# Hash masks of a fused attention kernel: 64-row products with zeros in place of 32-row products

## The chip, the cores and the metric

The kernel runs on one core of a Trainium2 chip. The metric is the device time in microseconds (us), the median of several runs. The engines are called as in the profile: PE is TensorE (PEld its weight loads), DVE is VectorE, ACT is ScalarE, POOL is GpSimd, and SP issues most DMA transfers.

## The reference

Two blocks follow each other. The first is attention with hash buckets: a query and a key meet only if the signs of six random projections agree. The second is a Fourier mixing with an MLP.

```python
q_bits = (einsum('bhsd,dk->bhsk', q, proj) > 0)       # 6 bits per query; the same for k
mask = q_bucket[:, :, :, None] == k_bucket[:, :, None, :]
scores = where(mask, q @ k.T / sqrt(D), -1e9)
attn = softmax(scores); x = attn @ v                  # heads side by side: (B, S, 512)
u = x + real(fft2(x)); un = layernorm(u)
out = u + relu(un @ w_ch1) @ w_ch2
```

Here B = 4, H = 8 heads, S = 768, D = 64, and all inputs are fp32, with 512 x 2048 and 2048 x 512 weights that arrive as 64-bit numbers and are narrowed on the chip.

## The kernel before

Heads are worked in pairs: pair `n` holds two heads on partitions 0 to 63 and 64 to 127, and there are 16 pairs, four for each batch. Queries and keys of a pair lie transposed in `qt` and `kt` (128 x 768). A pair is worked in six key chunks of 128 keys. For a chunk, `weigh` makes the scores for the two query halves `g` (384 queries each): two products on 64 rows of fp32, one for each head, into one of two PSUM buffers `sc` (L885), and the exponential on ACT into `pk` (L889), of which there are two. `values` multiplies the chunk before with the values into `oo` (L906). DVE adds up `pk` into `acc` (L980). After the last chunk, products with ones make the sums (L924), and `scale` divides: DVE turns the sums (L931), takes reciprocals, ACT copies them (L940), DVE turns back and multiplies (L941, L945).

Pairs 0 to 4, called LITE, get their mask on PE. `prepare` makes the sign bits of queries and keys in `qk`, bf16 (L794 products, L798 comparisons). The numbers are such that the product of query bits with key bits is zero where all six agree and hugely negative elsewhere, and it is added to the scores in PSUM by a product ahead of the score product (L878). Bits have 7 rows of use in a block of 32 partitions. Before, block `j` is query or key half `g = j // 2` of head `j % 2`, so the masks of half `g` for the two heads are two products on 32 rows each, at rows `64 g` and `64 g + 32`. Query bits are multiplied by 2**34 (L803). For the keys of the other half, two copies of 64 partitions exchange the blocks of the two halves (L806). The later pairs are masked on DVE by comparing bucket numbers (L895).

The order in each engine's queue is fixed in the program; each engine works its queue in order and waits at semaphores. The part up to the end of batch 0's attention and `pwf` (L1483) is in an order written by hand (a manual schedule). In batch 0, attention is interleaved with the arrival of the first weight matrix: each of 16 slices comes by DMA (`zraw`, `fraw`, L687) and is narrowed by DVE (L633, L637, L643) and ACT (L641, L648, L649); for half of them column means are made (`average`: `ws` L658, `part` L663, `wm` L666) and taken off (L672). From batch 1 on, attention is interleaved with the mixing of the batch before (`cs` L1078, `A` and `B` L1107) and its MLP (`h_p` L1382, `o` L1262). Pair 4 is the first of batch 1. `bt` L821 is the first step of pair 5's bits.

The preparation of pair `n + 1` is advanced one step in each chunk of pair `n` from the second on, so DVE works on bits between accumulation and conversion:

```python
for io, nm in enumerate("qk"):
    ps = pt([P, HALF], f"bits{nm}{n}")
    for j in range(4):
        g, h = divmod(j, 2)
        nc.tensor.matmul(ps[32 * j : 32 * j + 32, :], pjw[:, h * D : h * D + 32], ...)
```

Of the kernel before, what the change touches and what calls it, by code (L numbers as in the profile page):

```python
# [11 lines left out]
F32 = mybir.dt.float32  # L12
# [5 lines left out]
ALU = mybir.AluOpType  # L18
AX = mybir.AxisListType

P = 128
B, H, S, D = 4, 8, 768, 64
# [5 lines left out]
HALF = S // 2  # L28
# [10 lines left out]
BIG = 2.0**34  # L39
# [10 lines left out]
def _consts():  # L50


    s = np.arange(HALF)
    freq = np.concatenate([2 * np.arange(NK), 2 * np.arange(NK) + 1])
    ang = 2.0 * np.pi * (np.outer(s, freq) % S) / S
    seq = np.stack([np.cos(ang), np.sin(ang)])
    seq = seq.reshape(2, NT // 2, P, 2 * NK).transpose(2, 0, 1, 3)


    d = np.arange(DM // 2)  # L60
    ang = 2.0 * np.pi * (np.outer(d, np.arange(DM)) % DM) / DM
    sin = -np.sin(ang)
    sin[0] = 1.0 - 2.0 * (np.arange(DM) % 2)
    chan = np.concatenate([np.cos(ang), sin]).reshape(NDC, P, DM).transpose(1, 0, 2)

    off = np.zeros((P, 2))
    for h in range(2):
        off[h * D : h * D + NBITS] = 0.5  # L70
        off[h * D + NBITS] = (NBITS / 4.0, -1.0)


    pw = np.zeros((P, 2, P))
    for r in range(P):
        h, bit = divmod(r % 32, NBITS)
        if h < 2:
            pw[r, h] = 2.0**bit


    d = np.arange(DM // 2)
    fr = np.concatenate([np.arange(DM // 2 + 1), np.arange(1, DM // 2)])
    ang = 2.0 * np.pi * (np.outer(d, fr) % DM) / DM
    ch = np.where(np.arange(DM) <= DM // 2, np.cos(ang), np.sin(ang))
    ch = ch.reshape(2, P, DM // 2, 2).transpose(1, 0, 3, 2)

    s = np.concatenate([np.arange(2, HALF // 2, 2), np.arange(1, HALF // 2, 2)])  # L90
    rows = np.concatenate([s, [0, HALF // 2], s])
    kind = np.repeat([0, 1, 2, 3], [len(s), 1, 1, len(s)])
    sq = np.zeros((2, 2, P, HALF + 1))
    for par in range(2):
        cols = slice(par * NK, HALF + 1 if par else NK)
        ang = 2.0 * np.pi * (np.outer(rows, freq[: HALF + 1][cols]) % S) / S
        for k in range(2):
            own = kind == (0 if par == k else 3)
            own |= (kind == 1) & (k == 0) | (kind == 2) & (k == par)
            w = np.where(own[:, None], np.sin(ang) if k else np.cos(ang), 0.0)  # L100
            w = w.reshape(NT // 2, P, -1)
            sq[0, k, :, cols] = w[0 if par == k else 2]
            sq[1, k, :, cols] = w[1]
    sq = sq.transpose(2, 0, 1, 3)
    return {
        "pw": np.ascontiguousarray(pw, dtype=np.float32),
        "ch": np.ascontiguousarray(ch, dtype=np.float32),
        "sq": np.ascontiguousarray(sq, dtype=np.float32),
        "seq": np.ascontiguousarray(seq, dtype=np.float32),
        "chan": np.ascontiguousarray(chan, dtype=np.float32),  # L110

        "off4": np.ascontiguousarray(np.tile(off[:32], (4, 1)), dtype=np.float32),
        "off": np.ascontiguousarray(off, dtype=np.float32),
    }

# [366 lines left out]
def _main(  # L482
# [13 lines left out]
    nc = tc.nc  # L496

    const = ctx.enter_context(tc.tile_pool(name="const", bufs=1))
# [39 lines left out]
    def load(n, names="qkv", second=nc.sync):  # L538

        b, t = divmod(n, NPAIR)
        for nm in names:
            src = {"q": q, "k": k, "v": v}[nm]
            tag, bufs = ("vn", 2) if nm == "v" else ("qkn", 2)
            tl = wt([P, S], F32, tag, f"{nm}n{n}", bufs)
            nat[nm, n] = tl
            if nm == "v" or n == 0:  # L550
                tc_ = tl.rearrange("p (c h d) -> p c h d", c=NT, h=2)
                for h in range(2):
                    s = src[b, 2 * t + h]
                    s = (
                        s.rearrange("(p c) d -> p c d", c=NT) if nm == "q"
                        else s.rearrange("(c p) d -> p c d", p=P)
                    )
                    (second if h else nc.sync).dma_start(tc_[:, :, h, :], s)
                continue
            for i in range(4):  # L560
                s = src[b, 2 * t + i // 2, :, i % 2 * 32 : i % 2 * 32 + 32]
                d = tl[32 * i : 32 * i + 32]
                if nm == "k":
                    nc.sync.dma_start(
                        d.rearrange("p (j a) -> p j a", a=32),
                        s.rearrange("(j b) a -> b j a", b=32),
                    )
                else:
                    s = s.rearrange("(j b r) a -> r b j a", b=32, r=2)
                    d = d.rearrange("p (r j a) -> r p j a", r=2, a=32)  # L570
                    for r in range(2):
                        nc.sync.dma_start(d[r], s[r])
# [14 lines left out]
        nc.sync.dma_start(pjw[h * D : (h + 1) * D, h * D : h * D + NBITS], proj)  # L587
    off = const.tile([P, 2], F32, tag="off", name="off")
    nc.sync.dma_start(off, cn["off4"].ap())
    load(0, "v")  # L590
    pj = const.tile([P, 32], F32, tag="pj", name="pj")
    nc.gpsimd.memset(pj, 0.0)
# [156 lines left out]
    def prepare(n):  # L749
# [3 lines left out]
        for io, nm in enumerate("qk"):  # L753
            tn = nat.pop((nm, n))
            tt = wt([P, S], F32, nm + "t", f"{nm}t{n}")
            if n > 0:
                to, at = tt, tn
                if nm == "q":

                    to = tt.rearrange("p (i r n) -> p r i n", i=2, r=2)  # L760
                    at = tn.rearrange("p (r i n) -> p r i n", i=2, r=2)
# [21 lines left out]
        if lite:  # L783

            qk = wt([P, 2, S], BF16, "qb", f"qkb{n}")
            bits = {"q": qk[:, 0, 0:HALF], "k": qk[:, 1, 0:HALF]}
            for io, nm in enumerate("qk"):  # L790
                ps = pt([P, HALF], f"bits{nm}{n}")
                for j in range(4):
                    g, h = divmod(j, 2)
                    nc.tensor.matmul(  # L794
                        ps[32 * j : 32 * j + 32, :], pjw[:, h * D : h * D + 32],
                        ts[nm][:, g * HALF : (g + 1) * HALF], start=True, stop=True,
                    )
                nc.vector.tensor_scalar(  # L798
                    bits[nm], ps, 0.0, off[:, io : io + 1],
                    op0=ALU.is_gt, op1=ALU.subtract,  # L800
                )
                if io == 0:
                    nc.vector.tensor_scalar(bits[nm], bits[nm], BIG, None, op0=ALU.mult)  # L803
                else:
                    for g in range(2):
                        nc.vector.tensor_copy(  # L806
                            qk[g * D : (g + 1) * D, 1, HALF:S],
                            qk[(1 - g) * D : (2 - g) * D, 1, 0:HALF],
                        )
                yield  # L810
            preps[n] = ts["q"], ts["k"], qk, None
            return
# [50 lines left out]
    def weigh(n, c):  # L863

        qt, kt, qb, kb = preps[n]
        ks = slice(c * P, (c + 1) * P)
        heads = [slice(h * D, (h + 1) * D) for h in range(2)]
        pk = pks[npk[0] % NPK]
        npk[0] += 1
        for g in range(2):  # L870
            qs = slice(g * HALF, (g + 1) * HALF)
            ps = ps_sc.tile([P, 2, 512], F32, tag="sc", name=f"sc{n}_{g}_{c}")
            if kb is None:

                at = (c + (NT // 2 if g else 0)) % NT * P
                for h in range(2):
                    rows = slice(g * D + 32 * h, g * D + 32 * h + 32)
                    nc.tensor.matmul(  # L878
                        ps[:, h, 0:HALF], qb[rows, 1, at : at + P], qb[rows, 0, 0:HALF],
                        start=True, stop=False,  # L880
                    )

            for h, rows in enumerate(heads):
                with behind() if g + h and n >= NPAIR else nullcontext():
                    last[0] = nc.tensor.matmul(  # L885
                        ps[:, h, 0:HALF], kt[rows, ks], qt[rows, qs],
                        start=kb is not None, stop=True,
                    )
            nc.scalar.activation(  # L889
                pk[:, g, :, 0:HALF], ps[:, :, 0:HALF], AF.Exp, scale=SCALE  # L890
            )
        if kb is not None:
            for h in range(2):
                w = pk[:, :, h, 0:HALF]
                nc.vector.scalar_tensor_tensor(  # L895
                    w, qb[:, h].rearrange("p (g s) -> p g s", g=2), kb[:, h, c : c + 1], w,
                    op0=ALU.is_equal, op1=ALU.mult,
                )
        return pk
# [260 lines left out]
    at = NR * 2 * P  # L1160
# [425 lines left out]
```

## Time and profile before

| | |
|---|---|
| time, median of 3 runs | 1102.68 us (1102.34 to 1106.73) |
| profiled execution, span from first to last instruction | 1100.83 us |
| its own time around the span | not recorded apart; the median of the runs is 1.85 us above the span |
| PE busy | 1054.5 us, 96% of the span |
| DVE busy | 786.5 us, 71% |
| ACT busy | 500.6 us, 45% |
| mask products L878 | 120, of 331 ns each, first at 11.0 us, last at 152.3 us |
| score products L885 | 768 records, two passes for one fp32 product |
| granted PE clock | 0.995 of full |

Busy time is the union of the records of an engine. On PE the start of a record is where it began to stream, while its end is modelled and overlaps the next one; so steps between starts are the time that a product costs, and a busy PE is not a PE at its peak. Idle time ahead of an instruction is put down to the semaphore that came last.

### The profile page before, as it was taken

To read this page: it belongs to the slowest core of one execution; us is meant where nothing else is said; L and a number is where in the kernel's file an instruction comes from. 1 tells how busy PE (TensorE), PEld (TensorE's weight loads), DVE (VectorE), ACT (ScalarE), POOL (GpSimd) and SP (SyncE) were. 2 spreads that over 40 slices of the span, in tenths; PEclk is the share of its full clock that TensorE was granted. 3 is DMA by queue.
4 is the path that set the end of the run, shared out by engine and by line. 5 is a ranking of instruction groups with operands and counts; after the bars stand their busy time and mean duration, and the time that the engine had idled before them with its cause. 6 is when DMAs were issued, how large, how long until landed. Compare 5 with 4: busy or idle time off the path is not lost.

```text
span 1100.8 us, 14127 instructions
## 1 busy us (share of the span) xinstructions
PE 1054.5 (96%) x4933; PEld 629.4 (57%) x4933; DVE 786.5 (71%) x1321; ACT 500.6 (45%) x1055; POOL 58.6 (5%) x132
## 2 busy tenths in 40 slices
PE   7999997999989999999999999999999999999996
PEld 2333354446744675545664576645674569768675
DVE  5798958868699977776767785965856785644353
ACT  6888555653276324454326433355315522340420
POOL 0000000002000020010000011001000002100000
PEclk9999999999999999999999999999999999999998
DMA  8745443441056161322144134213032205122401
GB/s 224 221 90 119 76 123 88 149 147 26 20 139 210 46 204 34 66 61 70 26 157 108 48 73 162 44 39 96 15 121 75 68 24 172 54 82 85 126 20 41
DMA packets 175566, 103.13 MB, mean 94 GB/s; under 512 B 129408, under 2 KB 162816, under 8 KB 175488
## 3 DMA queue, kind: packets, MB, share of 16 engines
q1 hardware_dynamic: 169696, 88.65, 29.9%
q0 software_dynamic: 4224, 13.11, 3.8%
q8 instruction: 41, 0.67, 0.3%
q10 hardware_dynamic: 1568, 0.39, 0.2%
q14 instruction: 37, 0.30, 0.1%
HBM read 81.14 MB, written 20.97 MB: 93 GB/s over the span
## 4 chain that ended last, share of the span: by engine, by line
PE 63%; DVE 11%; ACT 4%; DMA 2%; issue 2%; DVEq 0%; SPq 0%; ACTq 0%
PE o L1262 22%; PE h_p L1382 21%; PE oo L906 7%; PE sc L885 6%; DVE pk L895 3%; PE cs L1078 2%; PE A L1107 2%; DMA zraw<-in_moe_w_ch_dram 2%; PE B L1107 1%; DVE acc L980 1%; ACT rr L940 1%; PE bits L817 1%; DVE w L1274 1%; DVE h L1248 1%; PE un L1133 1%
## 5 line engine op out<-in xcount | busy, mean ns | idle before, releaser
L1262 PE MATMUL o<-w,h 128*128 128x256 f32 x1152 | 259.4, 382 | 1.2 <-ACT tq L1281 0.7
L1262 PEld LDWEIGHTS o<-w,h 128*128 128x128 f32 x1152 | 216.3, 190 | 43.6 <-issue 4.6
L889 ACT ACTIVATE pk<-sc 128x768 f32<-128x768 f32 x192 | 148.5, 809 | 81.6 <-PE sc L885 64.5
L1382 PE MATMUL h_p<-x,w 128*128 128x384 f32 x448 | 163.1, 494 | 3.2 <-ACT h L1404 1.7
L885 PE MATMUL sc<-qt,kt 64*128 64x384 f32 x768 | 159.8, 519 | 5.4 <-ACT pk L889 5.1
L906 PE MATMUL oo<-pk,vn 128*64 128x385 f32 (+1 forms) x768 | 155.1, 499 | 4.0 <-DVE pk L895 3.3
L895 DVE SCALAR_TENSOR_TENSOR pk<-qb,kb,pk 128x768 f32<-128x768 bf16 x132 | 129.0, 1013 | 29.5 <-ACT pk L889 29.4
L1382 PEld LDWEIGHTS h_p<-x,w 128*128 128x128 f32 x448 | 82.0, 190 | 70.6 <-ACT pk L889 5.4
L980 DVE TENSOR_TENSOR acc<-acc,pk 128x1536 f32<-128x1536 f32 (+1 forms) x72 | 105.8, 1483 | 6.1 <-ACT pk L889 5.4
L1382 PE MATMUL h_p<-w 128*128 128x384 f32 x288 | 105.5, 489 | 2.3 <-ACT w L1419 2.3
L906 PEld LDWEIGHTS oo<-pk,vn 128*64 128x64 f32 x768 | 49.1, 136 | 97.8 <-issue 68.7
L885 PEld LDWEIGHTS sc<-qt,kt 64*128 64x128 f32 x768 | 62.9, 185 | 56.1 <-issue 29.6
L1382 PEld LDWEIGHTS h_p<-w 128*128 128x128 f32 x288 | 53.7, 190 | 41.7 <-ACT w L1419 3.5
L1292 ACT COPY tq<-o 128x256 f32<-128x256 f32 x24 | 8.9, 373 | 105.1 <-PE o L1262 105.1
L1274 DVE SCALAR_TENSOR_TENSOR w<-o,rs,w 128x256 f32<-128x256 f32 x56 | 26.8, 479 | 41.6 <-PE o L1262 41.6
L1262 PE MATMUL o<-w 128*128 128x256 f32 x176 | 42.3, 383 | 1.4 <-DVE w L1274 1.3
L1408 DVE TENSOR_TENSOR h<-h 128x384 f32<-128x384 f32 x32 | 17.8, 556 | 32.2 <-ACT h L1407 32.2
L1281 ACT COPY tq<-o 128x256 f32<-128x256 f32 x24 | 8.9, 371 | 69.3 <-PE o L1262 69.2
L1262 PEld LDWEIGHTS o<-w 128*128 128x128 f32 x176 | 32.8, 190 | 8.8 <-DVE w L1274 3.0
L1016 POOL DMA_DIRECT2D out_dram<-w x30 | 16.4, 548 | 388.8 <-issue 293.2
L1415 DVE TENSOR_TENSOR h<-h 128x384 f32<-128x384 f32 x32 | 17.7, 553 | 26.9 <-ACT h L1414 26.8
L1308 DVE TENSOR_TENSOR tq<-tq,o 128x256 f32<-128x256 f32 x24 | 10.0, 418 | 34.7 <-PE o L1262 34.7
(170 smaller groups left out, 1329.1 us busy)
## 6 DMA issues: line engine op xcount, KB each, us to landing
w<-ad SPq DMA_DIRECT2D x168, 128.0 KB, 2.0
w<-bd SPq DMA_DIRECT2D x42, 512.0 KB, 4.5
zraw<-in_moe_w_ch_dram POOLq DMA_DIRECT2D x16, 512.0 KB, 4.1
bd<-w SPq DMA_DIRECT2D x14, 512.0 KB, 4.2
vn<-in_v_dram SPq DMA_DIRECT2D x32, 192.0 KB, 3.4
qn<-in_q_dram SPq DMA_DIRECT2D x120, 48.0 KB, 2.4
kn<-in_k_dram SPq DMA_DIRECT2D x60, 96.0 KB, 3.4
zraw<-in_moe_w_ch_dram SPq DMA_DIRECT2D x8, 512.0 KB, 5.7
```

The costliest lines, as they stand in the source:

```text
L885: last[0] = nc.tensor.matmul(ps[:, h, 0:HALF], kt[rows, ks], qt[rows, qs], start=kb is not None, stop=True,)
L889: nc.scalar.activation(pk[:, g, :, 0:HALF], ps[:, :, 0:HALF], AF.Exp, scale=SCALE)
L895: nc.vector.scalar_tensor_tensor(w, qb[:, h].rearrange("p (g s) -> p g s", g=2), kb[:, h, c : c + 1], w, op0=ALU.is_equal, op1=ALU.mult,)
L906: nc.tensor.matmul(oos[g][h * D : (h + 1) * D, 0:w], nat["v", n][:, (2 * c + h) * D : (2 * c + h + 1) * D], pk[:, g, h, 0:w], start=(c == ...
L980: nc.vector.tensor_tensor(acc[:, g], (first if c == 1 else acc)[:, g], new[:, g], op=ALU.add,)
L1078: nc.tensor.matmul(ps[:, pc + 2 * lo : pc + 2 * hi - 1 : 2], z[:, cp, pc, par, t * P : (t + 1) * P], ch[:, cp, pc, lo:hi], start=(cp == 0) ...
L1107: nc.tensor.matmul(ps[:, cols], F[:, par, k, t, j * P : (j + 1) * P], sq[:, t, k, cols], start=(t == 0), stop=(t == 1),)
L1262: nc.tensor.matmul(ps, a[:, r], right7[i][:, r], start=start and r == 0, stop=r == HF // 2 - 1, skip_group_check=not start,)
L1274: nc.vector.scalar_tensor_tensor(t[:, cols], src, r, t[:, cols], op0=ALU.mult, op1=ALU.add)
L1382: nc.tensor.matmul(ps, left[:, k], right[i][:, k], start=start and k == 0, stop=k == 1, skip_group_check=not start,)
L1408: nc.vector.tensor_tensor(c21, c12, c21, op=ALU.add)
L1415: nc.vector.tensor_tensor(c22, c21, c22, op=ALU.add)
```

## The change

The blocks of bits are ordered by head and then by half: block `j` is half `j % 2` of head `j // 2`. A head's two halves now lie on the 64 rows that also hold the head's queries and keys. The mask product of half `g` runs on these 64 rows; the query bits exist twice, `qz[:, 0]` and `qz[:, 1]`, and in version `g` the block of the other half is zero. A new constant `own` (128 x 2, holding 2**34 or 0) is loaded once by SP and is the per-partition scalar of the multiplications: two instead of one for a pair. The exchange of key halves is now between neighbouring blocks of 32 partitions, in four copies instead of two. The comparisons, the number of products and the exponentials are as before.

```diff
+        "own": np.where(np.arange(P)[:, None] // 32 % 2 == np.arange(2), BIG, 0.0),
...
+    own = const.tile([P, 2], F32, tag="own", name="own")
+    nc.sync.dma_start(own, cn["own"].ap())
     load(0, "v")
...
             qk = wt([P, 2, S], BF16, "qb", f"qkb{n}")
-            bits = {"q": qk[:, 0, 0:HALF], "k": qk[:, 1, 0:HALF]}
+            qz = qk[:, 0].rearrange("p (g s) -> p g s", g=2)
+            bits = {"q": qz[:, 0], "k": qk[:, 1, 0:HALF]}
...
-                    g, h = divmod(j, 2)
+                    h, g = divmod(j, 2)
...
                 if io == 0:
-                    nc.vector.tensor_scalar(bits[nm], bits[nm], BIG, None, op0=ALU.mult)
+                    for g in (1, 0):
+                        nc.vector.tensor_scalar(
+                            qz[:, g], qz[:, 0], own[:, g : g + 1], None, op0=ALU.mult
+                        )
                 else:
-                    for g in range(2):
-                        nc.vector.tensor_copy(
-                            qk[g * D : (g + 1) * D, 1, HALF:S],
-                            qk[(1 - g) * D : (2 - g) * D, 1, 0:HALF],
-                        )
+                    for j in range(4):
+                        to, at = (slice(32 * i, 32 * i + 32) for i in (j, j ^ 1))
+                        nc.vector.tensor_copy(qk[to, 1, HALF:S], qk[at, 1, 0:HALF])
...
-                for h in range(2):
-                    rows = slice(g * D + 32 * h, g * D + 32 * h + 32)
+                for h, rows in enumerate(heads):
                     nc.tensor.matmul(
-                        ps[:, h, 0:HALF], qb[rows, 1, at : at + P], qb[rows, 0, 0:HALF],
+                        ps[:, h, 0:HALF], qb[rows, 1, at : at + P],
+                        qb[rows, 0, g * HALF : (g + 1) * HALF],
                         start=True, stop=False,
                     )
```

More of the change, by code (lines that the diff above doesn't have):

```diff
@@ L112, in _consts @@
         "off4": np.ascontiguousarray(np.tile(off[:32], (4, 1)), dtype=np.float32),
+        "own": np.ascontiguousarray(
+            np.where(np.arange(P)[:, None] // 32 % 2 == np.arange(2), BIG, 0.0),
+            dtype=np.float32,
+        ),
         "off": np.ascontiguousarray(off, dtype=np.float32),
```

## The prediction

> **What bounds the kernel now.** I read the page first, for the stage that the change touches. The masked hash products (`L878`) run from 11.0 to 152.3 us of a span of 1100.8, which is slices 1 to 6 of 40.
>
> ```profile
> PE   7999997999989999999999999999999999999996
> ...
> DVE  5798958868699977776767785965856785644353
> ACT  6888555653276324454326433355315522340420
> ```
>
> TensorE (PE) looks full there, but so nearly are ScalarE (ACT, slices 1 to 3) and VectorE (DVE, slices 2 to 3 and 5). Busy time in three windows cut at the events that matter below (window, length, PE, PE weight loads, DVE, ACT) says the same:
>
> ```profile
> 11.00:41.60 30.60, 29.42 (x174) 9.80 (x175) 20.83 (x35) 24.95 (x44) 0.00 (x0) 1.00 0.84 264
> 41.60:95.60 54.00, 52.37 (x317) 17.48 (x316) 48.18 (x76) 48.31 (x96) 0.00 (x0) 1.00 0.50 96
> 95.60:141.70 46.10, 43.76 (x257) 15.77 (x257) 43.59 (x78) 27.85 (x60) 0.11 (x1) 1.00 0.50 111
> ```
>
> From 41.6 to 95.6 three engines share the bound: 52.4, 48.2 and 48.3 of 54.0 us. From 95.6 to 141.7 DVE has 43.6 of 46.1. So the next question is what the PE time is made of; the PE timeline of one key chunk shows it (start, length, group):
>
> ```profile
> 17.13 0.34 PE L878 MATMUL sc<-qkb 32*128 32x384 bf16 x2
> 17.40 0.92 PE L885 MATMUL sc<-qt,kt 64*128 64x384 f32 x4
> 18.25 0.34 PE L878 MATMUL sc<-qkb 32*128 32x384 bf16 x2
> 18.51 0.92 PE L885 MATMUL sc<-qt,kt 64*128 64x384 f32 x4
> 19.36 1.51 PE L906 MATMUL oo<-pk,vn 128*64 128x385 f32 x8
> 20.80 0.34 PE L878 MATMUL sc<-qkb 32*128 32x384 bf16 x2
> ```
>
> A chunk takes 3.67 us: mask pair 0.27, scores 0.85, mask pair 0.26, scores 0.85, values 1.44. Starts are to be trusted, ends overlap. Last, the timelines of DVE and PE, for the places where DVE waits for PE (what PE can give it back) and PE for DVE. The bracket is the idle time before, and its releaser:
>
> ```profile
> 65.11 2.48 DVE L672 TENSOR_TENSOR w<-w,wm 128x512 f32<-128x512 f32 x4 [0.75 <-PE wm L666]
> ...
> 70.23 0.58 DVE L931 STREAM_TRANSPOSE rt<-sum 128x384 f32<-128x384 f32 x1 [0.75 <-PE sum L924]
> ...
> 95.66 0.58 DVE L931 STREAM_TRANSPOSE rt<-sum 128x384 f32<-128x384 f32 x1 [2.30 <-PE sum L924]
> ...
> 121.16 0.98 DVE L941 STREAM_TRANSPOSE rt<-rr 128x768 f32<-128x768 f32 x1 [1.73 <-ACT rr L940]
> ...
> 141.70 1.16 PE L1078 MATMUL cs<-ch,z 128*128 128x127 f32 x8 [1.42 <-DVE bt L821]
> ```
>
> Those four are all the waits over 0.15 us that DVE has from 40.68 to 141.64. At 141.70 PE waits for a DVE queue that has run through since 121.16. This is the ceiling of the whole change.
>
> [...] Inside the 128x128 stream of `L1107` (groups of four passes at 168.89, 169.54, 170.19) a pass of 192 columns takes 0.65/4 = 0.163 us, while the step from its last pass into the 64-row scores takes 0.256: 0.095 of drain. [...] each pass has its own 128-row load, recorded at 190 ns, and still follows in 0.163 us. [...] no 64-row bf16 product runs here. [...]
>
> **The change part by part.**
>
> *TensorE, per chunk.* The counts stay: 120 mask products, two concurrent per half, in 30 chunks. What goes are mode changes, since mask and scores are now both 64 rows by 128. Before, mask to first score pass is 0.262 (0.160 of columns, the rest drain and load); the first score pass takes 0.427 instead of 0.320, since its fp32 weights (0.107 between the two loads of a head) can't be loaded ahead of the change; last pass to next mask is 0.415 (0.320 and 0.095). After: 0.163, 0.323, 0.323 for the first half and 0.163, 0.323, 0.415 for the second, which still leaves the mode for the values; 0.007 more for the first load. Scores and masks of a chunk fall from 2.22 to 1.72, so 0.50 us. Thirty chunks offer 15 us on PE.
>
> *DVE, per pair.* The tile listing gives the prices.
>
> ```profile
> L806 DVE COPY qkb<-qkb x10: 253/255/256, 11.0 to 118.1; 64x384 bf16<-64x384 bf16 x10
> L798 DVE TENSOR_SCALAR qkb<-bitsq,off x5: 611/612/619, 9.5 to 110.5; 128x384 bf16<-128x384 f32 x5
> L803 DVE TENSOR_SCALAR qkb<-qkb x5: 259/260/261, 10.2 to 111.2; 128x384 bf16<-128x384 bf16 x5
> ```
>
> One multiplication more (0.26, with its wait 0.29) and two copies more (2 x 0.255; a copy of 32 partitions has the same 384 elements each): 0.80 per pair, 4.0 in five pairs. [...] the bound is the 0.61 of `L798`, which also takes a per-partition scalar: 0.70 more per pair. Below, an op of 384 elements has no reason to get cheaper than 0.26. I take 0.26.
>
> *SP.* One transfer more (`own`, 1 KB) ahead of `load(0, "v")`. Its neighbour `off` has a 587 ns issue and lands 4.1 us later, so `own` lands near 8.4 and is needed at 10.2. Behind it the value loads, `zraw` and the loads of pair 1 are each issued up to 0.6 later. ACT waits 1.06 for a `zraw` at 23.25, so 0 to 0.6 us is lost; the queue is blocked later anyway (a `qn` issue at 10.19 takes 2.95), I take 0.2. ACT, POOL and the order on PE are unchanged.
>
> *Where the 15 us go.*
> 1. 11.0 to 31.4: the first mask starts 0.30 later (one multiplication ahead of the key bits), its second half waits for four copies, not two; with the cheaper products the scores are ready as before. From 13.36 to 31.39 ACT runs through but for that DMA wait: exponentials and weight conversion, 3.6 us per chunk against PE's 3.67 before. PE only waits more: gain 0.
> 2. 31.4 to 40.68: here ACT idles for PE (0.62, 0.30, and 1.67 until `part` L663). Two chunks in a row are PE's: 0.6 at `part`, 1.1 at the sum that releases DVE at 40.68.
> 3. 40.68 to 95.66: DVE could give back 0.75 + 0.75 + 2.30 = 3.8 and gets 1.6 more work. ACT is tighter. It passes on some 0.65 at `part` 60.41 (the long wait there, 3.42, ends with a PE product that waited 0.92 for DVE `L798`), then 0.19 + 0.17 + 0.31 + 0.30 = 0.97 of waits for PE up to 89.1, and one chunk of PE alone, 0.5. So the sum arrives about 2.0 earlier. DVE would be ready at 93.35 - 1.1 + 0.8 = 93.05, the sum comes at 93.66: 2.0.
> 4. 95.66 to 141.70: DVE runs through, with the ACT round trip of 1.73, which moves along. Nine chunks save 4.5 us on PE and all of it becomes waiting: for `pk`, which DVE frees late, and at `L1078`, whose 1.42 grows. Pair 4's 0.8 is fully exposed: 2.0 - 0.8 = 1.2.
> 5. After 141.70: the last two chunks, at 142.79 and 151.16, are PE's: 1.0. Everything later depends on triggers that move along.
>
> Sum 1.2 + 1.0 - 0.2 = 2.0 us. Against the span of 1100.83 that is 1098.8. The median of the runs lies 1.85 above the span (start and end around it), so **1100.7 us**. A measurement can tell about 0.5%, 5.5 us, from no change.
>
> **The rivals.**
> *DVE and ACT give way (faster).* For it: PE is busy nearly throughout. Against: DVE's waits. If DVE's 3.8 of waits, the 1.73, 1.1 before and 1.0 after are all taken and 2.4 for pairs 2 to 4 paid, that is 5.2 us: 1097.5. More needs DVE to stop being last at 141.70; then up to 15: 1088.
> *Mask products get no cheaper (slower).* If the change from bf16 to fp32 drains as the change of rows does, or the scores' load waits for the mask on the same rows, PE saves nothing. Then DVE's added work decides. Pair 0 adds 0.30 at the start; pairs 1 to 3 fit into DVE's waits; pair 4 adds 0.80 ahead of 141.70; `own` 0.2. That is +1.3: 1104.0, with a slow multiplication +2.3. It decides once PE saves less than 0.8/6 = 0.13 per chunk. Against it: no drain shows within a mode in `L1107`; but both operand types are fp32 there.
> *The two heads' products run one after another (weaker gain).* 60 halves by 0.16 is 9.6 us more on PE, which leaves 5.4 of the 15, 0.18 per chunk: just past that point, about 1103. Against: the 64-row scores of two heads start 7 ns apart.
> *The rows don't change.* Excluded: the products in the changed kernel's instruction order are on 64 rows, all else but the named parts in the same order.
>
> **How the numbers follow.** Forecast 0.65, its own range 1098.5 to 1102.7 (loss at SP 0 to 0.6, slow multiplication, ACT giving back 1 more or less). First rival 0.15, of which 0.10 beyond 5.5 us. No saving 0.17, of which 0.06 beyond 5.5 us, where mask products even become dearer. Serial heads 0.03. So faster 0.10, same 0.84, slower 0.06. The range takes in the first rival's ceiling and the second's price: 1097.0 to 1104.5.
>
> **What would show it.** Right: mask to score about 0.17 and a chunk's products 0.50 shorter; more PE idle before `L878` and at `L1078`; DVE's waits at `L931` shorter; 141.70 moved by about 1. Wrong: mask to score still 0.26 (rival two), or `L1078` reached without a wait for DVE and several us earlier (rival one).

## The result, and the profile after

The changed kernel takes 1102.14 us (median of 20 runs, 1099.91 to 1104.45) beside 1102.88 us for the kernel before (20 runs): a ratio of 0.9993, interval 0.9984 to 1.0002. A second set of runs of it (`e12c_after_again`, below) gives 0.9996, 0.9983 to 1.0009. That is no difference that the measurement can tell: from 1.8 us faster to 0.2 slower, and the forecast gain of 2.0 lies just outside. The span of the profiled execution fell from 1100.8 to 1100.4 us.

TensorE did become cheaper. On the page PE's busy time falls from 1054.5 to 1043.3 us, and slices 3 and 5 of its row are 8 where 9 stood before:

```profile
PE   7989897999989999999999999999999999999996
...
DVE  5899958878599977776767785965856785644353
ACT  6987555553276324454326433355315522340420
```

The three windows of the prediction in the changed kernel (window, length, PE, weight loads, DVE, ACT):

```profile
11.00:41.60 30.60, 27.71 (x188) 11.51 (x186) 24.13 (x44) 25.56 (x45) 0.00 (x0) 1.00 0.92 274
41.60:95.60 54.00, 48.45 (x326) 18.75 (x324) 51.18 (x87) 49.57 (x100) 0.00 (x0) 1.00 0.54 107
95.60:141.70 46.10, 38.87 (x251) 16.60 (x250) 41.82 (x76) 25.61 (x57) 0.11 (x1) 0.99 0.49 107
```

In the middle window PE goes from 52.4 to 48.5 of 54.0 us, DVE from 48.2 to 51.2. PE now has over 5 us to spare there, and the two others have fewer than 5. PE's timeline of the chunk that the prediction showed (start, length, group, idle time before and its releaser):

```profile
17.80 0.34 PE L885 MATMUL sc<-qkb 64*128 64x384 bf16 x2 [0.48 <-ACT pk L897]
17.96 0.82 PE L893 MATMUL sc<-qt,kt 64*128 64x384 f32 x4
18.60 0.34 PE L885 MATMUL sc<-qkb 64*128 64x384 bf16 x2
18.76 0.82 PE L893 MATMUL sc<-qt,kt 64*128 64x384 f32 x4
19.52 1.51 PE L914 MATMUL oo<-pk,vn 128*64 128x385 f32 x8
21.39 0.34 PE L885 MATMUL sc<-qkb 64*128 64x384 bf16 x2 [0.36 <-ACT pk L897]
```

From mask to score 0.16 us, and from the first mask to the values 19.52 - 17.80 = 1.72, as against 2.22. The step to the next chunk is still 3.59 (before 3.67): most of the half microsecond has become waiting for ACT, 0.36 at 21.39. The tile listing of the bits (min/median/max ns, first and last start):

```profile
L885 PE MATMUL sc<-qkb x120: 319/323/357, 11.9 to 151.2; 64*128 64x384 bf16 x120
L817 DVE COPY qkb<-qkb x20: 247/252/256, 11.9 to 116.1; 32x384 bf16<-32x384 bf16 x20
L811 DVE TENSOR_SCALAR qkb<-qkb,own x10: 319/320/321, 10.6 to 108.6; 128x384 bf16<-128x384 bf16 x10
```

And the waits, from the timelines of DVE and PE:

```profile
39.53 0.58 DVE L939 STREAM_TRANSPOSE rt<-sum 128x384 f32<-128x384 f32 x1 [2.43 <-PE sum L932]
...
92.78 0.58 DVE L939 STREAM_TRANSPOSE rt<-sum 128x384 f32<-128x384 f32 x1
...
119.15 0.98 DVE L949 STREAM_TRANSPOSE rt<-rr 128x768 f32<-128x768 f32 x1 [1.73 <-ACT rr L948]
```

```profile
139.69 1.16 PE L1086 MATMUL cs<-ch,z 128*128 128x127 f32 x8 [1.93 <-DVE bt L829]
```

The wait of 2.30 us at 92.78 is gone, and so are the two of 0.75: DVE has given back what it had. The ACT round trip of 1.73 moved along unchanged. PE reaches `L1086` earlier and waits longer for DVE, 1.93 instead of 1.42.

How much earlier the same instruction starts than in the kernel before, at the milestones of the prediction (the first row is a start of the masks, the rest starts of the named instruction):

| milestone, us before | forecast | measured | again, in `e12c_after_again` |
|---|---|---|---|
| first mask, 11.02 | +0.30 | +0.89 | +1.05 |
| `part` 60.41 | -0.65 | -1.15 | -1.15 |
| sums turned, 95.66 | -2.0 | -2.88 | -2.9 |
| `cs` 141.70 | -1.2 | -2.01 | -2.00 |
| PE at 156 | -2.2 | -1.25 | -1.28 |
| PE from 350 on | -2.0 | -0.9 | -1.0 |

So the attention stage gave somewhat more than forecast up to 141.70, and between there and 350 us over half of it was lost again, in both traces.

### The profile page after: what moved, and what is told of

Same layout as the page of the kernel before. It is cut to its first block, busy times and chain, and to the rows that moved or that the text cites. A ratio compares the mean times of both kernels' runs of the same rounds, so it can differ in the third digit from the quotient of the medians.

```text
span 1100.4 us, 14144 instructions
## 1 busy us (share of the span) xinstructions
PE 1043.3 (95%) x4933; PEld 632.7 (57%) x4933; DVE 790.5 (72%) x1336; ACT 499.5 (45%) x1055; POOL 58.6 (5%) x132
## 4 chain that ended last, share of the span: by engine, by line
PE 61%; DVE 11%; ACT 4%; DMA 2%; issue 2%; DVEq 0%; SPq 0%; ACTq 0%
PE o L1270 22%; PE h_p L1390 20%; PE oo L914 6%; PE sc L893 6%; DVE pk L903 3%; PE cs L1086 2%; DMA zraw<-in_moe_w_ch_dram 2%; PE A L1115 2%; PE B L1115 1%; DVE acc L988 1%; ACT rr L948 1%; DVE w L1282 1%; DVE h L1256 1%; PE bits L825 1%; PE un L1141 1%
## 5 line engine op out<-in xcount | busy, mean ns | idle before, releaser
L893 PE MATMUL sc<-qt,kt 64*128 64x384 f32 x768 | 155.7, 508 | 6.0 <-ACT pk L897 5.7
L914 PE MATMUL oo<-pk,vn 128*64 128x385 f32 (+1 forms) x768 | 155.3, 499 | 6.0 <-DVE pk L903 3.0
L914 PEld LDWEIGHTS oo<-pk,vn 128*64 128x64 f32 x768 | 49.1, 136 | 100.0 <-issue 69.3
L893 PEld LDWEIGHTS sc<-qt,kt 64*128 64x128 f32 x768 | 66.9, 188 | 51.3 <-issue 24.0
L1282 DVE SCALAR_TENSOR_TENSOR w<-o,rs,w 128x256 f32<-128x256 f32 x56 | 26.7, 478 | 41.6 <-PE o L1270 41.6
L1086 PE MATMUL cs<-ch,z 128*128 128x128 f32 (+3 forms) x192 | 33.2, 324 | 3.0 <-DVE bt L829 1.9
```

The source lines that it names most:

```text
L893: last[0] = nc.tensor.matmul(ps[:, h, 0:HALF], kt[rows, ks], qt[rows, qs], start=kb is not None, stop=True,)
L914: nc.tensor.matmul(oos[g][h * D : (h + 1) * D, 0:w], nat["v", n][:, (2 * c + h) * D : (2 * c + h + 1) * D], pk[:, g, h, 0:w], start=(c == ...
L1086: nc.tensor.matmul(ps[:, pc + 2 * lo : pc + 2 * hi - 1 : 2], z[:, cp, pc, par, t * P : (t + 1) * P], ch[:, cp, pc, lo:hi], start=(cp == 0) ...
L1282: nc.vector.scalar_tensor_tensor(t[:, cols], src, r, t[:, cols], op0=ALU.mult, op1=ALU.add)
```

## The experiments

**Theory.** PE's saving is whole, but DVE and ACT give out a chunk at the old pace, so PE only waits. **Rivals.** PE saves less than the starts suggest (drains or loads elsewhere); DVE's added work eats the gain; the loss after 141.70 has a cause of its own.

### Both other engines relieved

Both kernels with the same cuts: DVE without the subtraction of the mean and without the accumulation of chunks 2 to 4 in batch 0, ACT without the two range checks for the first matrix.

```diff
-            nc.vector.tensor_tensor(w, w, avg, op=ALU.subtract)
...
+        if col < NDC * DFF // WC:
+            return
         nc.scalar.activation(t, hi, AF.Abs)
...
+                elif b == 0:
+                    for g in (0, 1) if c == 1 else ():
...
```

> The kernel before, with DVE and ACT work of the masked stage left out: the column means are not taken off the first weight matrix (L672), the accumulation of chunks 2 to 4 in batch 0 is left out, and so are the two range checks of ACT (L648, L649) in the conversion of the first matrix. The output is not the reference's. It is the base for the next run. Ceiling theory (PE's saving is real, DVE and ACT cap it): PE becomes the only bound up to 141.7 us, so the stage shortens by PE's waits there, some 3 to 5 us. Work theory (the added DVE work eats the saving): the same.

> The changed kernel with the same work left out. Ceiling theory: against the run before it, 10 to 15 us faster (30 chunks of 0.50 us, less the start of pair 0), where the full kernels differ by 0.7. Work theory (products no cheaper end to end, or DVE's 4 us eat them): at most 3 us faster.

Measured: 1099.08 us (0.9971 of the kernel before, 0.9961 to 0.9982) with 32 rows and 1084.37 us (0.9859, 0.984 to 0.9879) with 64. The change is worth 14.7 us between these two medians; the kernel with 64 rows has only five runs, one of which took 1090.39. Between their traces the lead grows evenly: 4.6 us at 54, 8.7 at 90, 11.9 at 127. At 155, behind the last mask, it is 12.8, of the 15 us that the prediction had on offer; at 184 it is 12.9. The 1.1 more at 190 are not the masks' saving: there the trace with 32 rows has a stretch at half clock (184.54; more on this below) that the other does not have. PE's timeline with 64 rows (first line of three chunks in a row) has steps of 3.16 us, 0.5 under the old chunk, and no idle time:

```profile
62.20 0.34 PE L886 MATMUL sc<-qkb 64*128 64x384 bf16 x2
...
65.36 0.34 PE L886 MATMUL sc<-qkb 64*128 64x384 bf16 x2
...
68.52 0.34 PE L886 MATMUL sc<-qkb 64*128 64x384 bf16 x2
```

The windows from 41.6 to 95.6 of the two, 32 rows first, then 64:

```profile
41.60:95.60 54.00, 54.00 (x328) 18.03 (x326) 36.73 (x64) 35.30 (x67) 0.00 (x0) 1.00 0.50 105
```

```profile
41.60:95.60 54.00, 54.00 (x372) 21.09 (x372) 44.31 (x81) 39.54 (x79) 0.11 (x1) 1.00 0.61 138
```

PE is full in both and gets through 372 records of products instead of 328. The saving per chunk is real and whole, which ends the first rival. The relief itself is worth only 3 us to the kernel before, but 18 to the changed one: with 32 rows PE is the bound, with 64 rows the work that was taken away.

### DVE relieved alone

The same pair with ACT's checks left in.

> The kernel before with DVE's part of the work of e1 left out alone (column means not taken off, accumulation of chunks 2 to 4 in batch 0 left out; the output is not the reference's); ACT's range checks stay. Base for the next run. Ceiling theory: 2 to 4 us faster than before, PE's waits of the stage.

> The changed kernel with the same DVE work left out. It tells which engine caps PE. If DVE alone is the cap: 12 to 15 us faster than e9c, as e2 was than e1. If ACT alone: below 2 us, as in the full kernels. If ACT caps up to 95 us and DVE from there to 141.7, as the prediction's steps have it: nine chunks of 0.5 in the second part come free and the first part stays, so 5 to 8 us faster than e9c, with a lead of 2 to 3.5 us at 95 us.

Measured: 1101.32 us (0.9992, 0.998 to 1.0005) and 1097.3 us (0.9957, 0.9942 to 0.9973). The change is worth 4.0 us here (as an estimate from 12 and 11 runs, 1.4 to 5.8), against 14.7 with ACT relieved too and 0.5 to 0.7 with neither. The expectations were missed: the relief of the kernel before is worth 1.0, not 2 to 4, and 4.0 lies between the cases "ACT alone" and "ACT, then DVE". Between the two traces the lead is 5.2 us at 95, where the last case had 2 to 3.5, and 6.2 at 141.70. So most of what this relief frees comes before 95 us, and DVE was a cap there too, not ACT alone.

The middle window, without and with the change, and PE's waits up to 142 us in the second (engine, line, releaser: us in total, times, longest) show what is left:

```profile
41.60:95.60 54.00, 53.32 (x321) 17.89 (x320) 36.10 (x63) 49.31 (x98) 0.00 (x0) 1.00 0.51 102
41.60:95.60 54.00, 50.07 (x340) 20.03 (x342) 40.33 (x72) 50.90 (x109) 0.11 (x1) 1.00 0.57 122
```

```profile
PE sc L884 <- ACT pk L896: 6.1, 8, 1.9
PE oo L913 <- ACT pk L896: 2.1, 1, 2.1
PE sc L884 <- DVE qkb L804: 1.3, 1, 1.3
PE wm L672 <- ACT part L669: 1.1, 1, 1.1
```

DVE has 14 us free, ACT is busy for 50.9 of 54, and nine waits of 8.2 us are for exponentials. The 2.1 at `L913` comes from a DMA: ahead of that exponential in ACT's queue stands the squaring of pair 5's queries, for which ACT waits:

```profile
107.66 0.84 ACT L749 ACTIVATE sq<-qn 128x768 bf16<-128x768 f32 x1 [4.94 <-DMA qn<-in_q_dram]
```

So work was taken off two engines before the saving came through, and DVE alone was not enough. ACT relieved alone was not tried, and some of what ACT holds back here is a wait for a transfer, not work of its own.

### DVE's added work alone

The kernel before with 32-row products, and on DVE the second multiplication and the four copies of 32 partitions.

```diff
+                    nc.vector.tensor_scalar(qk[:, 0, HALF:S], bits[nm], BIG, None, op0=ALU.mult)
                     nc.vector.tensor_scalar(bits[nm], bits[nm], BIG, None, op0=ALU.mult)
...
-                    for g in range(2):
...
+                    for j in range(4):
...
```

> The kernel before with 32-row products and DVE's added instructions alone: a second multiplication into the unused half of the query bits, and four key copies of 32 partitions in place of two of 64. Output unchanged. Ceiling theory: the chain of DVE that PE meets at 141.7 us comes 0.8 to 1.5 us later, the time rises by 1 to 1.5 us. Theory that DVE's work is hidden: both within 0.3 us of before. Copies of 32 partitions: 0.255 us each like those of 64.

Measured: 1102.99 us, 1.0006 (0.9999 to 1.0013), which cannot be told from no change; the 1 to 1.5 us were not seen in the time. Between the traces, from 35 to 108 us nothing is later (-0.19); from 119 on it is 0.64 later. So 0.83 us are exposed at pair 4, which is the 0.80 that rival two had priced, and the work of pairs 1 to 3 is hidden. From 350 us on this trace, of the slowest of its 21 runs, is 2.3 late: it has stretches at half clock, at 174.81 and 188.47, that the trace of the kernel before lacks.

### Taking that work off DVE

Three ways: multiplications and copies of pairs 1 to 4 on POOL, only the copies on POOL, and pair 4's multiplications and copies on ACT.

```diff
-                        nc.vector.tensor_copy(qk[to, 1, HALF:S], qk[at, 1, 0:HALF])
+                        (nc.gpsimd if n else nc.vector).tensor_copy(qk[to, 1, HALF:S], qk[at, 1, 0:HALF])
...
+                        if n == 4:
+                            nc.scalar.activation(
+                                qz[:, g], qz[:, 0], AF.Copy, scale=own[:, g : g + 1]
...
```

> The changed kernel with the two multiplications and four copies of pairs 1 to 4 on POOL. Output unchanged. Ceiling theory: DVE loses 1.57 us for each of pairs 2 to 4, and where DVE meets PE (139.7 us after the change) comes 1.5 to 3 us earlier; the time falls by 1 to 3 us. If ACT is the tighter cap before 95 us: by the 1.6 of pair 4 alone. If DVE's work is hidden: no difference. POOL's price is not known from the traces; up to 1 us for an instruction it stays ahead of the next pair.

> The changed kernel with only the four key copies of pairs 1 to 4 on POOL (0.50 us each there by e4, due a chunk later). Ceiling theory: pair 4's DVE work falls by 4 x 0.25 = 1.0 us, so PE meets DVE 0.7 to 1.0 us earlier near 139.7 us. Rival: POOL's copies take longer beside DVE and the next pair waits for them, as in e4: later by 0.5 or more at 35 and 92 us.

> The changed kernel with the two multiplications and four key copies of pair 4 alone on ACT, which stands idle there (4.9 us until 110.5, 3.1 until 117.5). Output unchanged. Ceiling theory: DVE's chain to 139.7 us loses 1.7 us of work, PE meets it 1.0 to 1.7 us earlier; time lower by about 1 us, 1101 us. Rival: ACT's instructions wait for DVE's bits and hold up the exponentials behind them: no gain there, or later.

The gains that the ceiling theory expected did not come. All three are slower than the kernel before: 1106.6 us (1.0038, 1.0022 to 1.0053), 1106.33 (1.0037, 1.0023 to 1.0052) and 1108.66 (1.0065, 1.0044 to 1.0087). From the tile listing of the first, what POOL takes:

```profile
L817 POOL COPY qkb<-qkb x16: 493/503/872, 33.9 to 122.2; 32x384 bf16<-32x384 bf16 x16
L811 POOL TENSOR_SCALAR qkb<-qkb,own x8: 1242/1942/3622, 29.1 to 118.3; 128x384 bf16<-128x384 bf16 x8
```

A multiplication takes 4 to 11 times DVE's 0.32 us, a copy 2 to 3.5 times its 0.25. The bits come late: up to 142 us PE waits three times for POOL's copies in each, 3.0 us in the first and 2.1 in the second. On ACT the prices are moderate (0.61 and 0.51 us), but the work stands in ACT's queue ahead of exponentials:

```profile
110.93 1.26 ACT L812 ACTIVATE qkb<-qkb,own 128x384 bf16<-128x384 bf16 x2 [5.73 <-DVE qkb L805]
112.10 1.49 ACT L904 ACTIVATE pk<-sc 128x768 f32<-128x768 f32 x2
...
119.25 2.07 ACT L822 COPY qkb<-qkb 32x384 bf16<-32x384 bf16 x4 [4.83 <-DVE qkb L805]
121.34 0.81 ACT L904 ACTIVATE pk<-sc 128x768 f32<-128x768 f32 x1
```

ACT waits 5.73 and 4.83 us for DVE's comparison, while the scores behind are ready; PE waits 3.31 and 4.41 us for those exponentials. Within pair 4 this execution falls 7.8 us behind the changed kernel (2.7 late before it, 10.5 after), which is the sum of these two waits. The 2.7 come from before pair 4, which alone was changed: they are there by 31 us, with a stretch at half clock at 27.60.

### Other work off DVE

In both kernels four of the eight late subtractions (`L672` before, `L678` after), the ones ahead of 141.70, go to POOL.

```diff
-            nc.vector.tensor_tensor(w, w, avg, op=ALU.subtract)
+            (eng if c > 1 else nc.vector).tensor_tensor(w, w, avg, op=ALU.subtract)
```

> The kernel before, with four of the eight subtractions of late column means (L672, batch 1, 121 to 136 us) on POOL instead of DVE: DVE loses 4 x 0.68 = 2.7 us in its closed stretch ahead of 141.7. Output unchanged. Ceiling theory: PE waits there 1.42 us for DVE, so it can gain at most about 1.4, then PE's own work bounds: 0.7 to 1.5 us earlier at that place. If DVE is no ceiling: no change. From e4, POOL takes 1.2 to 3.6 us for one instruction of 384 elements, so four take at most some 15 us and may just be late for the first use near 138 us: then slower by up to 3.

> The changed kernel with the same four subtractions on POOL. Ceiling theory: PE waited 1.05 and 1.93 us for DVE in this stretch, so it gains up to 2.7 at 139.7 us, more than the kernel before gains by the same edit; time 1099.5 to 1101. If DVE is no ceiling: no change. If POOL is late: slower by up to 3.

Measured: 1107.92 us (1.0049, 1.0036 to 1.0062) and 1106.83 us (1.004, 1.0026 to 1.0055), both slower, and by more than the 3 us expected for a late POOL. The line `L678` of the second:

```profile
L678 POOL TENSOR_TENSOR w<-w,mean x4: 1363/1582/1714, 123.3 to 127.8; 128x512 f32<-128x512 f32 x4
L678 DVE TENSOR_TENSOR w<-w,mean x4: 677/1216/1755, 123.4 to 132.5; 128x512 f32<-128x512 f32 x4
```

DVE's own subtractions took 0.68 us everywhere else; beside POOL's they take up to 1.76, and PE waits 5.1 us for DVE at `L1086`. The two of DVE's subtractions that start beside POOL's take 1.76 us, the two after it 0.68; what slows them was not shown. The four take 4.9 us, where all eight took 5.4 (8 x 0.68). Another pair of DVE instructions in that time, `L1051`, takes 3.17 us where the changed kernel needs 1.02. Counted together, DVE spends 1.6 us more there with half of the subtractions gone than with all eight.

### What is lost after 141.70

Apart from the start and the last 9 to 10 us, the PE clock has stretches of 3.413 us at half speed: in this trace of the changed kernel at 140.97 and 188.75, in that of before only at 227.29. The windows around them, cut at the clock's own steps (columns: window, length, busy time of PE, weight loads, DVE, ACT and POOL with counts, then the granted clock, DMA share and GB/s), after first, then before:

```profile
110.25:113.66 3.41, 1.49 (x8) 0.40 (x8) 3.34 (x8) 2.88 (x6) 0.00 (x0) 1.00 0.11 17
...
137.56:140.97 3.41, 1.48 (x11) 1.06 (x10) 2.08 (x2) 1.22 (x4) 0.00 (x0) 1.00 0.75 235
140.97:144.38 3.41, 3.41 (x14) 2.44 (x14) 0.00 (x0) 2.04 (x6) 0.00 (x0) 0.50 0.67 188
185.34:188.75 3.41, 1.77 (x11) 1.06 (x13) 2.89 (x4) 3.19 (x6) 0.00 (x0) 1.00 0.00 0
188.75:192.16 3.41, 3.41 (x10) 1.45 (x9) 3.41 (x9) 2.15 (x5) 0.00 (x0) 0.50 0.00 0
222.88:226.29 3.41, 2.55 (x10) 0.89 (x10) 2.73 (x6) 0.66 (x2) 0.00 (x0) 1.00 0.98 380
226.29:229.71 3.42, 2.21 (x13) 1.39 (x12) 1.73 (x5) 2.45 (x5) 0.00 (x0) 1.00 0.84 339
```

```profile
182.93:186.34 3.41, 1.97 (x11) 0.98 (x11) 2.17 (x4) 2.03 (x10) 0.00 (x0) 1.00 0.58 161
186.34:189.75 3.41, 2.14 (x13) 1.30 (x15) 2.86 (x4) 3.41 (x6) 0.00 (x0) 1.00 0.00 0
223.88:227.29 3.41, 1.38 (x11) 0.70 (x10) 1.32 (x4) 1.72 (x3) 0.00 (x0) 1.00 1.03 416
227.29:230.71 3.42, 3.42 (x7) 1.89 (x6) 1.91 (x5) 1.23 (x3) 0.00 (x0) 0.50 0.37 152
```

Each half-clock window follows one in which PE worked little: 1.38, 1.48 or 1.77 us. But the reverse does not hold: the window at 110.25 has 1.49 us of work, and full clock follows. In these two traces, what follows also differs with where a wait lies on the grid. Both kernels wait 2.0 us near 226. Before, this falls into one window; in the changed kernel it falls over a border (2.55 and 2.21 us of work) and costs no clock. The wait of 2.7 us near 186 falls over a border in both and leaves 1.77 us of work on one side in the changed kernel, 1.97 and 2.14 in the kernel before. Between about 1.5 and 1.8 us of work both happen, and what decides there stays open. In a window at half clock in which PE is busy throughout, half of 3.41, 1.7 us, is lost (estimate, from the granted 0.50). The leads show about that: from -2.01 at 141.70 to -0.54 at 145, from -0.62 to +0.93 around 189; and the kernel before loses 1.7 at 227.

If that takes the gain back, filling the wait ahead of 141 should bring it back. `e7_after_warm` makes the bits of pair 5 three times over, which fills PE while it waits for `bt`:

```diff
-        for j in range(4):
+        for j in range(12 if n == 5 else 4):
+            j %= 4
```

> The changed kernel with the bits products of pair 5 (L825) made three times instead of once, the same result: 1.6 us more work on PE inside the 1.93 us in which it waits for DVE near 138 us. Clock theory (a long wait of PE halves its clock for 3.4 us, which cost 1.3 us after 141 us): no half clock from 141 to 144, the lead of 2.0 over the kernel before is still 2.0 to 2.6 at 156 us where it was 1.25; time 1 us lower. Rival (the half clock falls there by chance): half clock as before, lead at 156 us about 1.2, time the same or higher. If the added products are late for DVE: lead at 141 us below 2.0.

The wait is shorter and the clock stays up there, as the clock theory had it:

```profile
142.50 1.16 PE L1087 MATMUL cs<-ch,z 128*128 128x127 f32 x8 [0.64 <-DVE bt L830]
```

Against the changed kernel this execution gains 1.55 us from 141 to 153. But the total is 1101.86 us, 0.9991 (0.9981 to 1.0001): no gain that can be told. Nor is the lead at 156 us the 2.0 to 2.6 expected: this execution is level with the kernel before there. A wait of ACT for a DMA, 2.64 us until 24.84, and a window at half clock behind it, at 28.94, had put it 2.8 us behind the changed kernel, and the window at 189 stayed. Over all runs the mean granted clock is 0.9925, no higher than that of the changed kernel. The experiment shows what one such window costs, not that the kernel can be rid of them.

The changed kernel once more:

> The changed kernel as it is, on the same chip as e11c and as a second profile of it. Clock theory: where the half clock of 3.4 us lies changes from run to run, the places up to 141 us where DVE and ACT decide do not, apart from the start: the lead at 141.7 us over the kernel before is 1.5 to 2.5 us again, and the end between 0 and 2 us ahead.

1101.82 us, 0.9996 (0.9983 to 1.0009). The lead is 2.00 us at 141.70, and the last lead is 1.0, both as expected. The half clock comes at 140.76 again, so its place did not change there; another, twice as long, comes at 185.13.

## Why the prediction was right, point by point

The time, 1102.1 for 1100.7, and "no difference that can be told" came out within what was forecast. The mechanism was right: PE's saving, and where it turns into waiting. That the time came so near is in part luck, since errors of 0.9 us too little (steps 2 and 3) and 2 us too much (step 5) partly cancelled. The step that failed is the fifth.

- *TensorE, 0.50 us per chunk.* Held to the hundredth: 1.72 where 2.22 was. Once little else binds, 12.8 of the 15 us are there at 155 us. The 0.163 that the prediction gives a mask product on 64 rows was the author's estimate; measured is 0.16 from mask to scores, and it was 0.27 with 32 rows. In the kernel before, the first weight load of the scores starts at 17.39, beside their first product at 17.40, after 0.17 us in which no load ran; in the changed one it starts at 17.80, beside the mask product and 0.16 ahead of the scores. That the saving comes from the changes of row number between mask and scores is argued: the parts of a chunk fit it, but no run separates that from the number of rows itself. The 0.095 us that the prediction calls drain is a measured step of 0.256 less the time of its columns; that PE drains there was not shown. Rival two (no saving), the serial heads and DVE's work as the whole story are out.
- *DVE, 0.80 per pair.* A multiplication with the scalar from `own` takes 0.320, not 0.260: the work is 0.87 per pair (2 x 0.32 - 0.26 and 4 x 0.25 - 2 x 0.255). `e3_before_dve_work` is the check: there both multiplications have a constant and take 0.26. The bound of 0.61 was not needed. Where it lies was right: exposed at pair 4, hidden at pairs 1 to 3 (`e3_before_dve_work`).
- *SP, 0.2 lost.* Nothing was lost: ACT's wait for the same `zraw` is 0.30 instead of 1.06. But the time around the span, 1.85 in the prediction, is 1.83 in the median of the runs before and 1.96 with the change, so 0.1 of a shorter span does not show in the time; why is not known.
- *Step 1, no gain up to 31.4.* Held in kind, but the start is 0.89 late, not 0.30. PE reached full clock at 11.26 instead of 8.84 us in this execution, so the bits came 0.44 later; the rest is DVE's. It cost nothing: PE waits there anyway.
- *Steps 2 and 3, 2.0 at 95.66.* 2.88: 1.15 at `part` where 0.65 was taken, and chunks between. DVE gave back all 3.8 us that it had, which is the ceiling that the prediction gave for this stretch: with 1.15 from the stretch before and the work of pairs 2 and 3 off, 3.8 + 1.15 - 2 x 0.87 is 3.2. "ACT is tighter" was too strong: with DVE relieved alone the lead here is 5.2.
- *Step 4, 2.0 - 0.8 at 141.70.* 2.88 - 2.01 = 0.87 was lost, which is the added work as measured. DVE runs through, its only wait the 1.73 for ACT, and PE's wait grows at `L1086` (1.93) and at `L914` (2.06, for an exponential that stands behind ACT's wait of 4.91 for a transfer). As forecast, PE's savings in these chunks all became waiting.
- *Step 5, 1.0 more after 141.70, and "everything later depends on triggers that move along".* The last chunk did give its 0.5, from -0.75 to -1.25; that of the one before is hidden under the half clock. But the lead did not move along. Waits grew on PE, as the prediction said, and it priced a growing wait at zero. After some of these waits the clock was halved for 3.4 us. The changed kernel's trace has two such windows, that of before has one; 1.7 us is the difference. A wait for an exponential at 172.63, 2.09 us instead of 1.40, takes 0.7 more. Sum: -2.0 - 1.0 + 1.7 + 0.7 = -0.6; measured -0.9. In the second trace that wait is 0.87, which gives back 0.5, and the window at 185 is twice as long and costs 2.7: -2.0 - 1.0 + 1.7 + 2.7 - 1.7 - 0.5 = -0.8; measured -1.0. Why the wait at 172.63 differs is not known.

The mean granted clock of all runs supports this: 0.9945, 0.9949 and 0.9952 in three sets of the kernel before, 0.9939 and 0.9926 in two of the changed one. A thousandth of 1100 us is 1.1 us, so 0.7 to 2.9 us of clock, at most, are lost to more windows. What is missing is 2.3 to 2.5 us: 3.0 (2.0 at 141.70 and 1.0 from the last two chunks) less the 0.5 to 0.7 of the medians. All runs can also be compared at equal clock. The mean times, before and after, are 1104.0 and 1102.3 us at a granted clock of 0.992, 1104.1 and 1101.5 at 0.993, 1103.1 and 1102.6 at 0.994, 1102.0 and 1100.7 at 0.995. Fitted over the 88 and 34 runs whose clock is on record, from several chips, the changed kernel is 1.3 us faster at equal clock (estimate, 0.8 to 1.8), where the plain means differ by 0.3. So about 1 us goes with the clock; the rest of what is missing stays open over all runs. It was not shown by removal either: the one window taken away was replaced by another.

The rival "DVE and ACT give way" was the right ceiling. They gave 2.9 us up to 95.66; 5.2 with work taken off DVE alone, 8.8 with work taken off both. No version here that makes the whole output can be told to be faster than the kernel before: every other place tried for DVE's work (POOL, ACT) costs more than DVE. These slower kernels have more waits on PE and a lower mean clock too, 0.9892 to 0.9930.

## What to carry to other kernels

Before pricing a saving on the busiest engine, count the idle time of the engines that pass it its work and take back its buffers: here 15 us of saving met about 4 us of idle time on DVE, and 2.9 came through. Test it by relieving the others in both versions: the difference shows whether the saving is real (12.8 us by 155 us) and which engines hold it (only 4.0 of the total with DVE alone relieved). A wait that was added on TensorE was not free here even off the critical path: 1.93 us of it ahead of 139.69 were followed by 3.41 us at half clock. See where such a wait falls and what clock follows.

## What was not expected of the hardware

The clock of PE changed on a grid of 3.413 us. In the trace of the changed kernel it changes at 11.26, 140.97, 144.38, 188.75, 192.17 and 1093.29 us, which are 38, 1, 13, 1 and 264 times 3.413 apart; in that of the kernel before at 8.84, 227.30, 230.71 and 1094.28, 64, 1 and 253 times. In the first 400 us of the fourteen traces, cut at that grid, 14 windows have more than 1.97 us without a product, and each is followed by one at half clock. Below 1.6 us only two are, both themselves in a half-clock window. Between, both happen: of 47 windows 14 are followed by half clock, and even among those over 1.9 us only 8 of 14. So the idle time of a window alone does not tell what follows. Half clock followed 1.93 us of waiting inside one window (137.76 to 139.69, in the changed kernel); it did not follow 1.92 in the window at 110.25 of the same trace, nor 2.70 us over a border (184.90 to 187.61, in the kernel before).

A per-partition scalar on DVE cost 0.06 us over a constant for 128x384 bf16 (0.320 in the changed kernel against 0.260 in `e3_before_dve_work`, whether the result overwrites its input or not).

The two subtractions on DVE that started beside one on POOL took 1.76 us instead of 0.68 for 128x512 fp32 (`e6_after_centre`).
